# Raw-weight differences in a tile of their own from group 0 on, two eviction adds a group by DMA, two differences moved behind a sum

## The chip, the cores and the metric

One core of a Trainium2 chip. Its engines run side by side, each through its own list of instructions in order: TensorE (PE; its weight loads are shown as PEld), VectorE (DVE), ScalarE (ACT), GpSimd (POOL) and SyncE (SP). SP, ACT and POOL also issue DMAs. The metric is the device time of one execution in microseconds (us), here the median of several runs of the same kernel.

## What is computed

Attention with a window and a few global tokens, followed by a mixture of eight experts whose routing weights P are balanced by eight rounds of row and column normalisation:

```python
h = np.maximum(x @ w1[e], 0.0)     # x: 4352 x 512, w1[e]: 512 x 1024
ye = h @ w2[e]                     # w2[e]: 1024 x 512
out += P[:, e:e + 1] * ye          # over the eight experts
```

There are B = 8 batches with 544 rows each, so 4352 tokens reach the experts. The output is fp32, 4352 x 512. Products are made in fp16 with fp32 sums.

## The kernel before, in words

The first part, up to about 390 us, is the attention, the routing and, in the gaps, the first layer (x @ w1, ReLU) of experts 0 to 3, whose results are kept in DRAM as `hd`. The change does not touch it.

The second part is a loop over `units` (m, e): token groups m = 0 to 8 (eight of 512 tokens, one of 256), and in each group the experts in the order 4, 0, 5, 1, 6, 2, 7, 3. Units at even places are experts 4 to 7, whose first layer is still to do; at odd places stand experts 0 to 3, whose h is loaded from `hd` and scaled by P. Work goes in pairs: the even unit's turn runs its own second layer and, in between, the first layer of the even unit after it.

The second layer of a unit is seven products of half-size matrices in place of eight (`product(i, q)`, q = 1 to 7). `sums` makes what they need beside h itself on VectorE: part 0 and 1 are sums of quarters of h (tile s), part 2 is two differences written into h in place; products 6 and 7 read those differences, products 3 and 4 do not. Products 1 to 5 are summed over all experts of the group in fixed PSUM banks; products 6 and 7 of an even unit and of the odd unit after it share a rotating bank, which is then added into the group's output tile `o` by `add` (one quarter of `o` each). `add` is called at odd units for q = 6 and 7, and for all q when the group closes. The first expert pair sets its quarter of `o` with a scaling on ScalarE (L950), later ones add on VectorE (L952). `store` sends `o` out by POOL's queue.

The first layer comes in two forms. The plain one is `l1` (L819 to L827): weights `w1s`, 1 MB, in one of the two buffers of `wpool` with the tag w1e. The fast one (`Fast`, from group 2 on, experts 5, 6 and 7) also uses seven products in place of eight, in two halves p = 0 and 1; its weights `w1q` hold four raw blocks and three differences or sums of them, which are made once, written to DRAM (`w1c`), and loaded from there by every later group. `Fast.s1` and `Fast.s2` have one VectorE sum each, from PSUM to PSUM (L868, L875); `sums_x` makes differences of the scaled x.

Where the seven blocks of `w1c` are made is what the change is about. Before: for experts 6 and 7 a raw half is loaded by SP into a w1e buffer as an extra entry of the load sequence `wseq`, ahead of the w1s of units 10, 12, 14 and 16; `prep_w1` (four VectorE instructions) follows in the even units of group 1, and POOL writes the tile to `w1c`. For expert 5 the raw halves are loaded by POOL's queue into a tile of its own (`wq`, one buffer) at units 8 and 11 and are prepared in units 9 and 13. `load_w1` issues the next entry of `wseq` as soon as the entry two places before it is marked as used.

The scheduling of instructions is by hand: on each engine they stand in the order in which the loop records them. POOL has little else to do in this part: it issues the loads of the second-layer weights `w2c` for experts 2, 7 and 3 near 394 us, the loads and writes around `wq`, and the stores of `o`. SP issues, in each even unit, the loads of P rows (`pb`), of x (`xg`, once a group), of `h`, and of first-layer weights.

Of the kernel before, what the change touches and what calls it, by code (L numbers as in the profile page):

```python
# [9 lines left out]
FP16 = mybir.dt.float16  # L10
FP32 = mybir.dt.float32
AF = mybir.ActivationFunctionType
ALU = mybir.AluOpType
# [10 lines left out]
def kernel(  # L24
# [13 lines left out]
    nc = tc.nc  # L38

    B, H, Sl, Dh = q_l.shape  # L40
    Sg = q_g.shape[2]
    D, E = moe_w_gate.shape
    F = moe_w1.shape[2]
    P = 128
# [28 lines left out]
    WX = {5: 2, 6: 2, 7: 2}  # L73
# [18 lines left out]
    with tc.tile_pool(name="att_c", bufs=1) as att_c, \  # L92
# [161 lines left out]
        for so in range(NJ):  # L254
            for c0, n in ((W, P), (W + Sl, W // NJ)):
                nc.vector.tensor_copy(out=zsel[:, so, c0 : c0 + NJ * n].rearrange("p (x s) -> p x s", s=NJ)[:, :, so],
                                      in_=identity[:, 0:n])
# [330 lines left out]
        for s in range(HP, NU + 1):  # L588
            slot = s
            b, hp = divmod(s, HP)  # L590
# [101 lines left out]
    def tt(out, in0, in1, op):  # L692
        nc.vector.tensor_tensor(out=out, in0=in0, in1=in1, op=op)  # L693
# [14 lines left out]
    def fast(i):  # L708
        return i < NUN and units[i][0] < B and units[i][0] >= WX.get(units[i][1], B)

    wseq = [(i, p) for i in range(0, NUN, 2) for p in ((0, 1) if fast(i) else (None,))]
    for j, (e, p) in enumerate((e, p) for e in WX if e != 5 for p in range(2)):
        wseq.insert(next(k for k, w in enumerate(wseq) if w[0] == E + (2, 4, 6, 8)[j]), (e, "raw", p))
    raw = {}
    wnext = 0

    def load_w1(used):
        nonlocal wnext
        while wnext < len(wseq) and (wnext < 2 or wseq[wnext - 2] in used):
            i, *p = wseq[wnext]  # L720
            if p[0] is None:
                w = w1s[i] = wpool.tile([P, DP, F], FP16, tag="w1e", name="w1s")
                nc.sync.dma_start(out=w, in_=w1d[units[i][1] - NL])
            else:
                w = wpool.tile([P, 7, 2, 256], FP16, tag="w1e", name="w1q")
                if p[0] == "raw":
                    load_raw(i, p[1], w, nc.sync)
                    raw[wseq[wnext]] = w
                else:
                    nc.sync.dma_start(out=w, in_=w1c[units[i][1]][p[0]])  # L730
                    w1s[(i, p[0])] = w
            wnext += 1
            if wnext < 2:
                return

    def load_raw(e, p, w, eng):
        for o, r, k in ((0, 0, 0), (1, 0, 1), (3, 1, 0), (2, 1, 1)):
            f0 = 512 * r + 256 * p
            eng.dma_start(out=w[:, o], in_=w1d[e - NL][:, 2 * k : 2 * k + 2, f0 : f0 + 256])

    def prep_w1(ks=()):
        for k in ks or list(raw):
            w = raw.pop(k)
            for o, a, b, op in ((5, 0, 3, ALU.subtract), (3, 3, 2, ALU.add), (4, 3, 0, ALU.subtract),
                                (6, 1, 4, ALU.subtract)):
                tt(w[:, o], w[:, a], w[:, b], op)
            nc.gpsimd.dma_start(out=w1c[k[0]][k[2]], in_=w)
            used.add(k)

    def load_pb(*us):  # L750
        us = [i for i in us if i < NUN]
# [189 lines left out]
    def add(i, q, pm):  # L941
        m, e = units[i]
        nt = groups[m][1] // P // 2
        if m not in os_:
            os_[m] = ypool.tile([P, NJ, D], FP32, tag="y", name="o")
        for j, (r, d, sg) in enumerate(QUARTER[q]):
            o = os_[m][:, nt * r : nt * (r + 1), HD * d : HD * (d + 1)]
            p = pm[:, 0 : HD * nt].rearrange("p (t d) -> p t d", d=HD)
            if (q >= 6 and e == ORDER[1]) or (q in (3, 4) and j == 0):
                nc.scalar.mul(o, p, 1.0 / float(E))  # L950
            else:
                nc.vector.scalar_tensor_tensor(out=o, in0=p, scalar=sg / float(E), in1=o, op0=ALU.mult, op1=ALU.add)  # L952
# [130 lines left out]
    for i, (m, e) in enumerate(units):  # L1083
        if i == 2 * E - 2:
            wqx.close()
            fsp = ctx.enter_context(tc.tile_pool(name="fsp", bufs=1, reuse_waits="tile"))
        if i in (E, E + 3):
            k = (5, "own", int(i > E))
            own = wqp.tile([P, 7, 2, 256], FP16, tag="wq", name="wq")
            load_raw(k[0], k[2], own, nc.gpsimd)  # L1090
        if i == NUN - 1:
            last_pair(i)
        elif i % 2 == 0:
            alloc_h(i + 2)
            load_pbs(i)
            if (i + 4) % E == 0:
                load_x((i + 4) // E)
            load_h(i + 3)
            load_w1(used)
            if fast(i):  # L1100
                sums(i, 2, 4)
            if fast(i + 2):
                f = Fast(i + 2, 0)
                if fast(i):
                    product(i, 3)
                    f.s0()
                    product(i, 4)
                    f.s1()
                    sums_x(i + 2, (4,))
                    product(i, 5)  # L1110
                    product(i, 2)
                    f.s2()
                    sums(i + 1, part=(1,))
                    sums(i + 1, part=(0, 2))
                else:
                    f.s0()
                    product(i, 3)
                    f.s1()
                    scale_h(i + 1, HF, HF + 2)
                    for q in (4, 5, 2):  # L1120
                        product(i, q)
                    f.s2()
                    scale_h(i + 1, HF + 2, FT)
                    sums(i + 1)
                used.add((i + 2, 0))
                if fast(i):
                    scale_x(i + 4, 0, 2)
                else:
                    scale_x(i + 4)
                    scale_h(i + 3, 0, HF)  # L1130
                product(i, 1)
                f.s3()
                nrot = 0
                product(i, 6)
                product(i, 7)
                continue
            if i + 2 < NUN:
                sums(i + 1)
            else:
                n = groups[m][1]  # L1140
                h = hs[i + 1]
                s = ss[i + 1] = xsp.tile([P, HF, n], FP16, tag="xs", name="sl")
                tt(s, h[:, 0:HF, 0:n], h[:, HF:FT, 0:n], ALU.add)
            if m > 0:
                prep_w1()
            scale_x(i + 4)
            if m == 0:
                for e in {2: (2,), 4: (7,), 6: (3,)}.get(i, ()):
                    prep_w2c(e)
            sums_x(i + 4)  # L1150
            scale_h(i + 3, 0, HF if fast(i + 4) else FT)
            for fm in range(3):
                l1(i + 2, fm, ps_rot, rot())
            for q, fm in ((3, 3), (4, 4), (5, 5), (2, 6), (1, 7), (6, None), (7, None)):
                product(i, q)
                if fm is not None:
                    l1(i + 2, fm, ps_rot, rot())
                if closes(i):
                    add(i, q, fixed[q])
            used.add((i + 2, None))  # L1160
        else:
            if i >= E * B - 1:
                load_h(i + 4)
            load_w1(used)
            load_pbs(i)
            if fast(i + 1):
                f = Fast(i + 1, 1)
                late = fast(i - 1)
                if not late:
                    product(i, 3)  # L1170
                for q in (6, 7):
                    product(i, q)
                    add(i, q, fixed[q])
                if late:
                    scale_x(i + 3, 2, 4)
                    scale_h(i + 2, 0, HF)
                if late:
                    product(i, 3)
                f.s0()
                product(i, 4)  # L1180
                f.s1()
                sums_x(i + 3, (5,))
                product(i, 5)
                product(i, 2)
                sums(i + 1, 0, 2, part=(0, 1))
                f.s2()
                sums(i + 1, 0, 2, part=(2,))
                scale_h(i + 2, HF, FT)
                sums_x(i + 3, (7, 6))
                product(i, 1)  # L1190
                f.s3()
                used.add((i + 1, 1))
                nrot = 0
                continue
            if m > 0:
                sums(i + 1)
            if i in (E + 1, E + 5):
                raw[k] = own
                prep_w1((k,))
            for q in (6, 7, 3, 4, 5, 2, 1):  # L1200
                product(i, q)
                if q >= 6 or closes(i):
                    add(i, q, fixed[q])
                if q == 7 and m == 0:
                    sums(i + 1)
            if closes(i):
                store(m)
# [31 lines left out]
```

## Time and profile before

| | us |
|---|---|
| runs, median of 3 | 1034.1 (1033.37 to 1034.63) |
| profiled execution, device time | 1033.45 |
| its span in the profile | 1031.3 |
| PE busy | 1004.4 |
| DVE busy | 896.5 |
| ACT busy | 521.6 |
| POOL busy | 146.3 |

The granted TensorE clock is 0.998 of full speed over the span. From 400 to 1000 us the engines' busy times in stretches of 50 us are 49.0 to 50.0 for PE, 41.6 to 49.2 for DVE and 12.5 to 18.9 for ACT. Rows of the order of time give a start, the time covered, engine, line, operation, what is written and read, shape and count; in brackets stands the idle time of the engine before it and what ended it. A matmul's end is modelled in the profile, so consecutive matmuls overlap in it; distances between starts show the pace.

### The profile page before, as it was taken

How to read it: one execution, taken by the hardware profiler on the slowest of the kernel's cores; microseconds unless marked ns; L12 is line 12 of the kernel's file. 1: busy time of each engine (PE TensorE's matmuls, PEld its weight loads, DVE VectorE, ACT ScalarE, POOL GpSimd, SP SyncE). 2: the span in 40 equal slices, each digit the busy share in tenths (PEclk: the TensorE clock that was granted, in tenths of full speed). 3: DMA queues.
4: the chain of work that ended last, by engine and by line, in shares of the span. 5: the costliest groups of instructions: out<-in, count | busy, mean ns of one | idle time of the engine just before them, and what ended most of it. 6: DMA issues, size and time to landing. Idle time of an engine off the chain costs nothing.

```text
span 1031.3 us, 23197 instructions
## 1 busy us (share of the span) xinstructions
PE 1004.4 (97%) x9286; PEld 739.9 (72%) x9286; DVE 896.5 (87%) x1752; ACT 521.6 (51%) x1316; POOL 146.3 (14%) x237
## 2 busy tenths in 40 slices
PE   7899999999999999999999999999999999999998
PEld 4555555555555466777678878878878878888887
DVE  8688877877875768989889999999999999999996
ACT  7767888888886674322223334334333333433331
POOL 7442332423403002001100000000000000000000
PEclk9999999999999999999999999999999999999999
DMA  9897699989946989837866556555655645645650
GB/s 269 192 221 215 125 272 217 200 247 214 207 163 171 283 292 294 235 103 248 305 252 234 190 176 229 194 180 190 205 184 188 218 175 201 212 172 184 210 196 25
DMA packets 103499, 213.72 MB, mean 207 GB/s; under 512 B 34192, under 2 KB 68448, under 8 KB 92896
## 3 DMA queue, kind: packets, MB, share of 16 engines
q1 hardware_dynamic: 56928, 167.47, 47.5%
q0 software_dynamic: 43856, 35.14, 18.9%
q10 hardware_dynamic: 2608, 9.64, 2.4%
q8 instruction: 72, 1.18, 0.4%
q14 instruction: 35, 0.29, 0.1%
HBM read 174.41 MB, written 59.12 MB: 226 GB/s over the span
## 4 chain that ended last, share of the span: by engine, by line
PE 79%; DVE 9%; ACT 6%; issue 3%; DMA 2%; POOL 0%; SPq 0%; ACTq 0%; DVEq 0%; POOLq 0%
PE m L936 25%; PE ph L468 18%; PE pf L843 10%; PE pm L936 10%; PE ph L825 9%; ACT Pu L311 2%; DVE Pu L348 2%; DVE h L693 1%; PE pt L275 1%; ACT qbd L285 1%; DVE s L693 1%; DVE o L952 1%; PE ptw L359 1%; PE po L380 1%; ACT hT L471 1%
## 5 line engine op out<-in xcount | busy, mean ns | idle before, releaser
L468 PE MATMUL ph<-xT,w1e 128*128 128x512 f16 (+1 forms) x1152 | 259.8, 367 | 2.6 <-ACT hT L471 1.3
L936 PEld LDWEIGHTS <-h 128*128 128x128 f16 x2160 | 210.0, 98 | 35.7 <-DVE h L693 2.2
L936 PE MATMUL m<-w2c,s 128*128 128x256 f16 x1620 | 199.9, 273 | 0.0
L936 PEld LDWEIGHTS <-s 128*128 128x128 f16 x1620 | 158.2, 98 | 27.0
L468 PEld LDWEIGHTS <-w1e 128*128 128x128 f16 x1152 | 105.1, 98 | 97.9 <-issue 8.8
L827 ACT ACTIVATE h<-ph 128x512 f16<-128x512 f32 (+1 forms) x144 | 78.9, 550 | 152.3 <-PE ph L825 144.6
L693 DVE TENSOR_TENSOR h<-h,pb 128x2048 f16<-128x2048 f16 (+2 forms) x66 | 155.1, 2349 | 0.8 <-DMA h<-hd 0.8
L850 ACT ACTIVATE h<-pf 128x512 f16<-128x512 f32 x144 | 82.7, 596 | 123.2 <-PE pf L843 111.2
L693 DVE TENSOR_TENSOR s<-h 128x1024 f16<-128x1024 f16 (+2 forms) x178 | 127.7, 759 | 16.4 <-ACT h L827 8.6
L936 PE MATMUL m<-w2c,h 128*128 128x256 f16 x1080 | 138.2, 273 | 0.0
L825 PE MATMUL ph<-xs,w1s 128*128 128x512 f16 (+1 forms) x576 | 127.3, 355 | 1.5 <-DMA w1s<-w1d 1.5
L936 PE MATMUL pm<-w2c,h 128*128 128x256 f16 x1080 | 124.8, 273 | 0.5
L471 ACT ACTIVATE hT<-ph 128x512 f16<-128x512 f32 (+1 forms) x188 | 102.0, 558 | 38.2 <-PE ph L468 35.2
L843 PEld LDWEIGHTS <-w1q 128*128 128x128 f16 x1008 | 98.5, 98 | 11.9
L311 ACT ACTIVATE Pu<-ms,mx 128x160 f16<-128x160 f32 x224 | 93.3, 424 | 3.8 <-DVE mx L308 3.1
L473 DVE TENSOR_SCALAR hT<-ph 128x512 f16<-128x512 f32 x100 | 67.7, 687 | 28.1 <-PE ph L468 28.0
L693 DVE TENSOR_TENSOR h<-h 128x1024 f16<-128x1024 f16 (+1 forms) x178 | 91.7, 557 | 0.4
L693 DVE TENSOR_TENSOR xs<-xg,pb 128x1024 f16<-128x1024 f16 (+2 forms) x48 | 79.8, 1663 | 7.5 <-DMA pb<-pd 7.5
L825 PEld LDWEIGHTS <-w1s 128*128 128x128 f16 x576 | 56.2, 98 | 39.6 <-DMA w1s<-w1d 2.0
L955 POOL DMA_DIRECT2D out_dram<-o x8 | 6.1, 757 | 530.1 <-DVE o L952 530.1
L843 PE MATMUL pf<-xs,w1q 128*128 128x256 f16 x576 | 80.5, 272 | 0.0
L308 DVE CUSTOM_DVE_ANT_0 ms<-sc,mask 128x160 f32<-128x160 f32 x224 | 59.2, 318 | 9.6 <-PE sc L303 9.5
(168 smaller groups left out, 1248.2 us busy)
## 6 DMA issues: line engine op xcount, KB each, us to landing
h<-hd SPq DMA_DIRECT2D x32, 1024.0 KB
w1q<-w1c SPq DMA_DIRECT2D x36, 896.0 KB
hd<-hT SPq DMA_DIRECT2D x26, 1024.0 KB
w1s<-w1d SPq DMA_DIRECT2D x18, 1024.0 KB
pb<-pd SPq DMA_DIRECT2D x64, 256.0 KB
w2c<-in_moe_w_dram POOLq DMA_DIRECT2D x16, 512.0 KB, 22.2
out_dram<-o POOLq DMA_DIRECT2D x8, 1024.0 KB, 4.6
f<-in_q_l_dram SPq DMA_DIRECT2D x15, 512.0 KB
```

Source lines behind the costliest of these rows:

```text
L308: nc.vector.tensor_tensor_reduce(out=ms[:, ii, :], in0=sc[:, SW * ii : SW * (ii + 1)], in1=mask[:, mi, :], scale=-scale, scalar=BIG, op0=A ...
L311: nc.scalar.activation(out=d["Pu"][:, i, :], in_=ms[:, ii, :], func=AF.Exp, scale=-1.0, bias=d["mx"][:, i : i + 1], accum_out=d["sm"][:, i ...
L348: nc.vector.tensor_tensor(out=d["Pu"][:, i0:i1, 0:KW], in0=d["Pu"][:, i0:i1, 0:KW], in1=d["rs"][:, i0:i1].unsqueeze(2).to_broadcast([P, i1 ...
L468: nc.tensor.matmul(ph[:, 0:n], wts[e][:, dk, P * fm : P * (fm + 1)], xT[m][:, dk, :], start=(dk == 0), stop=(dk == DP - 1))
L471: nc.scalar.activation(out=hT[:, fm, 0:n], in_=ph[:, 0:n], func=AF.Relu)
L473: nc.vector.tensor_scalar(out=hT[:, fm, 0:n], in0=ph[:, 0:n], scalar1=0.0, scalar2=None, op0=ALU.max)
L693: nc.vector.tensor_tensor(out=out, in0=in0, in1=in1, op=op)
L825: nc.tensor.matmul(ph[:, 0:n], w1s[i][:, dk, P * fm : P * (fm + 1)], xss[i][:, dk, 0:n], start=(dk == 0), stop=(dk == DP - 1))
L827: nc.scalar.activation(out=hs[i][:, fm, 0:n], in_=ph[:, 0:n], func=AF.Relu)
L843: nc.tensor.matmul(bank[:, 256 * c : 256 * (c + 1)], self.w[:, self.sta[q], k, P * c : P * (c + 1)], self.mov[q][:, k], start=(first and c ...
L850: nc.scalar.activation(out=self.h[:, k : k + 2, 256 * c : 256 * (c + 1)], in_=bank.rearrange("p (k t) -> p k t", k=2), func=AF.Relu)
L936: nc.tensor.matmul(pm[:, HD * t : HD * (t + 1)], lhs[0][:, k, lhs[1] + P * t : lhs[1] + P * (t + 1)], w[:, k, q - 1, :], start=(k == 0 and ...
```

## The change

Three things change in the second part.

First, the raw halves of experts 5, 6 and 7 are all loaded by POOL's queue into the one tile `wq`, at units 0, 4, 6, 8, 10 and 12 (`RAW`), and are prepared at units 3, 5, 7, 9, 11 and 13, in the odd unit ahead of its products. The entries of `wseq` for raw halves, and the calls of `prep_w1` in even units, are gone. Three of the six preparations now lie in group 0.

Second, in groups 2 to 7 `add` for q = 6 and the experts at places 3 to 5 of the order is a scaling on ScalarE into a buffer `a` (one buffer, 128 x 2 x 256 fp32) and a DMA of POOL's queue that adds `a` into `o`. The places 3 to 5 are experts 1, 6 and 2; expert 6 stands at an even place, so there are two such DMAs a group.

Third, where a fast unit is followed by a fast pair, part 2 of `sums(i, 2, 4)`, two differences of h, stands behind `sums_x(i + 2, (4,))` instead of ahead of product 3. Nothing is changed in which products TensorE makes or in their order.

```diff
-    for j, (e, p) in enumerate((e, p) for e in WX if e != 5 for p in range(2)):
-        wseq.insert(next(k for k, w in enumerate(wseq) if w[0] == E + (2, 4, 6, 8)[j]), (e, "raw", p))
+    RAW = {0: (5, 0, 3), 4: (5, 1, 5), 6: (6, 0, 7), 8: (6, 1, 9), 10: (7, 0, 11), 12: (7, 1, 13)}
...
-                if p[0] == "raw":
-                    load_raw(i, p[1], w, nc.sync)
-                    raw[wseq[wnext]] = w
-                else:
-                    nc.sync.dma_start(out=w, in_=w1c[units[i][1]][p[0]])
-                    w1s[(i, p[0])] = w
+                nc.sync.dma_start(out=w, in_=w1c[units[i][1]][p[0]])
+                w1s[(i, p[0])] = w
...
-    def prep_w1(ks=()):
-        for k in ks or list(raw):
-            w = raw.pop(k)
-            for o, a, b, op in ((5, 0, 3, ALU.subtract), (3, 3, 2, ALU.add), (4, 3, 0, ALU.subtract),
-                                (6, 1, 4, ALU.subtract)):
-                tt(w[:, o], w[:, a], w[:, b], op)
-            nc.gpsimd.dma_start(out=w1c[k[0]][k[2]], in_=w)
-            used.add(k)
+    def prep_w1(i):
+        for e, p, u in RAW.values():
+            if u == i:
+                w = raw.pop((e, p))
+                for o, a, b, op in ((5, 0, 3, ALU.subtract), (3, 3, 2, ALU.add), (4, 3, 0, ALU.subtract),
+                                    (6, 1, 4, ALU.subtract)):
+                    tt(w[:, o], w[:, a], w[:, b], op)
+                nc.gpsimd.dma_start(out=w1c[e][p], in_=w)
...
-            if (q >= 6 and e == ORDER[1]) or (q in (3, 4) and j == 0):
+            if q == 6 and e in ORDER[3:6] and 2 <= m < B:
+                a = acp.tile([P, 2, HD], FP32, tag="a", name="a")
+                nc.scalar.mul(a, p, sg / float(E))
+                nc.gpsimd.dma_start(out=o, in_=a, accum_op=ALU.add)
+            elif (q >= 6 and e == ORDER[1]) or (q in (3, 4) and j == 0):
...
-        if i in (E, E + 3):
-            k = (5, "own", int(i > E))
-            own = wqp.tile([P, 7, 2, 256], FP16, tag="wq", name="wq")
-            load_raw(k[0], k[2], own, nc.gpsimd)
+            acp = ctx.enter_context(tc.tile_pool(name="acp", bufs=1, reuse_waits="tile"))
+        if i in RAW:
+            e1, p1, _ = RAW[i]
+            raw[(e1, p1)] = wqp.tile([P, 7, 2, 256], FP16, tag="wq", name="wq")
+            load_raw(e1, p1, raw[(e1, p1)], nc.gpsimd)
...
             if fast(i):
-                sums(i, 2, 4)
+                sums(i, 2, 4, part=(0, 1))
+                if not fast(i + 2):
+                    sums(i, 2, 4, part=(2,))
             if fast(i + 2):
...
                     f.s1()
                     sums_x(i + 2, (4,))
+                    sums(i, 2, 4, part=(2,))
                     product(i, 5)
...
-            if m > 0:
-                prep_w1()
+            prep_w1(i)
             scale_x(i + 4)
...
-            if i in (E + 1, E + 5):
-                raw[k] = own
-                prep_w1((k,))
+            prep_w1(i)
             for q in (6, 7, 3, 4, 5, 2, 1):
```

## The prediction

> **What bounds the kernel now.** I read the page's totals first, then busy time by stretch, then TensorE's order of time. From the page:
>
> ```profile
> span 1031.3 us, 23197 instructions
> PE 1004.4 (97%) x9286; PEld 739.9 (72%) x9286; DVE 896.5 (87%) x1752; ACT 521.6 (51%) x1316; POOL 146.3 (14%) x237
> ```
>
> VectorE at 87% could pass for a second bound, so I cut two neighbouring groups of 512 tokens out of the late part. Columns: busy us and count of PE, PEld, DVE, ACT, POOL, then clock, DMA share, GB/s.
>
> ```profile
> 546.00:620.48 74.48, 74.39 (x650) 63.13 (x649) 71.57 (x98) 27.39 (x48) 0.76 (x1) 1.00 0.57 195
> 620.48:694.96 74.48, 74.40 (x650) 63.12 (x649) 71.69 (x98) 27.40 (x48) 0.77 (x1) 1.00 0.58 196
> ```
>
> Both last 74.48 us, and PE lacks 0.09 us in each. VectorE lacks 2.8 to 2.9 us, yet it delays PE by next to nothing. So taking work from VectorE is worth only what PE loses by waiting, and the matmuls stay the same, in number and order. The whole question is how much PE waits after 365 us, and what new wait appears. I read each loss from start to start: a row's last start is its end less 0.27 us, the next is due 0.109 us later (24 matmuls in 2.78 us: 2.51 / 23).
>
> The large losses are the first matmuls of layer 1 in group 1 (PE, order of time):
>
> ```profile
> 485.74 2.46 PE L936 MATMUL m<-w2c,s 128*128 128x256 f16 x21
> 489.20 1.47 PE L825 MATMUL ph<-xs,w1s 128*128 128x512 f16 x6 [1.00 <-DMA w1s<-w1d]
> ...
> 505.72 2.78 PE L936 MATMUL m<-w2c,s 128*128 128x256 f16 x24
> 508.97 0.82 PE L825 MATMUL ph<-xs,w1s 128*128 128x512 f16 x3 [0.47 <-DMA w1s<-w1d]
> ```
>
> Due at 488.04 and begun at 489.20: 1.16 us. Due at 508.34 and begun at 508.97: 0.63 us. Together 1.8 us, both ended by the landing of w1s.
>
> The small ones come back in each of the six groups 2 to 7:
>
> ```profile
> 556.75 0.71 PE L936 MATMUL m<-w2c,h 128*128 128x256 f16 x5
> 557.54 0.72 PE L936 MATMUL pm<-w2c,h 128*128 128x256 f16 x5
> ...
> 586.81 0.60 PE L843 MATMUL pf<-xs,w1q 128*128 128x256 f16 x4
> 587.28 0.60 PE L843 MATMUL pf<-t,w1q 128*128 128x256 f16 x4
> 587.72 1.91 PE L936 MATMUL m<-w2c,s 128*128 128x256 f16 x16
> 589.50 0.70 PE L843 MATMUL pf<-xs,w1q 128*128 128x256 f16 x5
> ```
>
> 0.24, 0.03 and 0.03 us: 0.3 a group.
>
> **Part 1: raw weights leave SP's queue and PE's weight buffers.** Before, a raw half of w1 takes one of the two buffers that w1s uses. SP's DMA issues:
>
> ```profile
> 461.23 0.32 SPq L723 DMA_DIRECT2D w1s<-w1d  x1
> ...
> 484.23 0.33 SPq L723 DMA_DIRECT2D w1s<-w1d  x1
> ```
>
> The issue at 484.23 is for the matmuls due at 488.04. After, nothing raw stands between, so each w1s takes the buffer that comes free one unit pair earlier: this load goes out at 461.2, 27 us ahead. The longest such transfer in the chain of waits took 7.33 us:
>
> ```profile
> 501.60 7.33 DMA w1s<-w1d
> ```
>
> Both waits go: -1.8 us. SP also loses sixteen issues of raw loads, which only helps the loads behind them. What hides the w1s load is its lead of 27 us; without it the 1.8 us would stay.
>
> **Part 2: three of the six blocks of differences move into group 0.** A block is four VectorE instructions on one tile. Each of units 3, 5 and 7 gets a block ahead of its two additions from PSUM. VectorE there, with the idle time before an instruction in brackets, then the block (the row of w1q), and PE's first matmul into the bank that the closing additions free:
>
> ```profile
> 421.17 4.42 DVE L693 TENSOR_TENSOR h<-h,pb 128x4096 f16<-128x4096 f16 x1
> 425.67 0.69 DVE L952 SCALAR_TENSOR_TENSOR o<-pm,o 128x512 f32<-128x512 f32 x1
> 426.53 0.69 DVE L952 SCALAR_TENSOR_TENSOR o<-pm,o 128x512 f32<-128x512 f32 x1 [0.17 <-PE pm L936]
> 430.83 1.23 DVE L693 TENSOR_TENSOR s<-h 128x2048 f16<-128x2048 f16 x1 [0.67 <-PE m L936]
> 444.73 0.69 DVE L952 SCALAR_TENSOR_TENSOR o<-pm,o 128x512 f32<-128x512 f32 x1 [1.31 <-PE pm L936]
> 445.60 0.69 DVE L952 SCALAR_TENSOR_TENSOR o<-pm,o 128x512 f32<-128x512 f32 x1 [0.18 <-PE pm L936]
> 449.96 1.83 DVE L693 TENSOR_TENSOR s<-h 128x2048 f16<-128x2048 f16 x2 [0.74 <-PE m L936]
> 463.86 0.69 DVE L952 SCALAR_TENSOR_TENSOR o<-pm,o 128x512 f32<-128x512 f32 x1 [1.31 <-PE pm L936]
> 464.73 0.69 DVE L952 SCALAR_TENSOR_TENSOR o<-pm,o 128x512 f32<-128x512 f32 x1 [0.18 <-PE pm L936]
> 468.28 3.87 DVE L952 SCALAR_TENSOR_TENSOR o<-m,o 128x512 f32<-128x512 f32 x6
> ...
> 476.20 1.80 DVE L693 TENSOR_TENSOR w1q<-w1q 128x512 f16<-128x512 f16 x4
> ...
> 471.49 1.04 PE L936 MATMUL m<-w2c,h 128*128 128x256 f16 x8
> ```
>
> The gaps: 0.08 + 0.17 + 0.67 + 1.31 + 0.18 + 0.74 + 1.31 + 0.18 = 4.64 us. Without a gap an instruction starts 0.08 us before the last one ends (588.08 + 0.76 against a successor at 588.75, in part 3's rows), so eight filled gaps hold 5.3 us. Three blocks cost 3 x 1.72 = 5.2. If the weights are there, VectorE reaches the additions at 468.28 as before (0.1 us early). The first of these ends at 468.97, and PE needs its bank at 471.49: the cover is 2.5 us. Nearer in time, unit 3's two additions end 1.7 us later, at 428.1 and 428.9; PE needs their banks for the second and third product of layer 1 after unit 3's last matmul (430.81, the wait that ends at 430.83), each some 0.9 us long (six matmuls in 1.47 us above, four a product), so from 431.7 on.
>
> But the first block adds a wait, and VectorE stands in order behind it: the additions, s and h for the next units, xs. The raw half is loaded by POOL right behind six loads of w2c in the same queue. The view of w2c's loads, the stretch after their last landing, the view of the line that loads raw weights, and the row of DMA issues that writes a finished block out (KB, us to landing):
>
> ```profile
> L689 POOL DMA_DIRECT2D w2c<-in_moe_w_dram x6: 747/775/797, 394.4 to 398.1; - x6
> DMA to landing us min/median/max: 10.9/21.0/26.9
> ...
> 424.50:434.00 9.50, 9.50 (x78) 7.37 (x77) 8.58 (x12) 1.77 (x3) 0.00 (x0) 1.00 0.83 318
> ...
> L739 POOL DMA_DIRECT2D wq<-w1d x8: 702/721/732, 474.4 to 498.6; - x8
> DMA to landing us min/median/max: 2.7/4.4/6.6
> ...
> w1c<-wq POOLq DMA_DIRECT2D x2, 896.0 KB, 7.0
> ```
>
> The last w2c lands at 398.1 + 26.9 = 425.0. Call T the time at which the last of the four raw loads lands. VectorE is ready at 425.5, and the block's second instruction, 0.46 us on, needs that load. So VectorE loses T - 426.0, is 0.1 us less late at the closing additions, and PE loses T - 428.6 where that is positive. Bounds for T: 425.0 (they land with the last w2c) and 434, when SP's loads of this stretch, which hold the DMA engines at 0.83, are through. By the nearest row such loads take 2.7 to 6.6 us, median 4.4. I take 4.0, since they are queued already: T = 429.0, a loss of 0.4 us; the ends are 0 and 5.4. Unit 3's additions, 3.0 us later still, then end by 431.1 and 431.9, wanted from 431.7 and 432.6: in time. Units 5 and 7 have no such wait: POOL writes the block out and loads the next half in 7.0 + 6.6 us at most, and 19 us lie between blocks. In group 1 VectorE has three blocks fewer, 5.2 us, and makes up what is left.
>
> **Part 3: a third party for two additions a group.** For experts 1 and 2 of groups 2 to 7, 12 times in all (the third name in that slice, expert 6, stands at an even place, which never adds), ScalarE scales PSUM into a buffer and POOL adds it by DMA. VectorE loses 0.6 us each, ScalarE gains about the same:
>
> ```profile
> 576.60 1.28 DVE L952 SCALAR_TENSOR_TENSOR o<-pm,o 128x512 f32<-128x512 f32 x2
> 588.08 0.76 DVE L693 TENSOR_TENSOR h<-h 128x512 f16<-128x512 f16 x2
> 588.75 0.69 DVE L868 TENSOR_TENSOR pf<-pf,c 128x512 f32<-128x512 f32 x1
> 618.26 1.29 DVE L952 SCALAR_TENSOR_TENSOR o<-pm,o 128x512 f32<-128x512 f32 x2
> ...
> 578.32 0.57 ACT L859 COPY pf<-pf 128x512 f32<-128x512 f32 x1 [4.25 <-PE pf L843]
> ```
>
> ScalarE idles 4.25 us before its next copy, which covers it. The accumulating DMA isn't in the trace; the raw and w2c rows bound it by 2.7 and 26.9 us. I take 4.4, because POOL's queue is empty there and DMA share is 0.57. The same quarter is next added by VectorE at 618.26, 41 us after the first of two. Only near 26.9 would the single buffer hold ScalarE back for some 8 us at the second expert. VectorE runs about 0.25 us earlier (the second addition still waits for its matmul), enough for the 0.03 at 587.28.
>
> **Part 4: two differences behind a sum.** The pair at 588.08 (0.67 us) goes behind the sum at 588.75 and the t after it. PE waits for that sum at 589.50, so that 0.03 goes too; the differences feed only products 6 and 7, later, and the work behind them on VectorE starts no later. The 0.24 at 557.54 stays: its work starts from PE's own result. Parts 3 and 4: 6 x 0.06 = -0.4 us.
>
> **Sum.** -1.8 - 0.4 + 0.4 = -1.8 us. The profiled run is 1033.45 us, its span and 2.15 around it; that gives 1031.65. The median of the runs is 0.65 above it, so the forecast is 1034.1 - 1.8 = **1032.3 us**.
>
> **Rivals.** *The first half lands in time* (T up to 428.6): no loss, 1034.1 - 2.2 = 1031.9. For it: the least landing of the row, 2.7 us; against it: SP's loads at 0.83 share. *Halved rate*: the four loads alternate with SP's, take twice the least of the row, 5.4 us; T = 430.4, loss 1.8, 1033.7. The Trainium skill, "DMA: Bandwidth & Descriptors", section "Queues, rings and completion order", says each DMA engine takes turns packet by packet among its queues; by that rule T depends on packet sizes, and no quoted row shows the turns. *Slower*: the loads come after SP's transfers, T = 434, at VectorE's first block in unit 3; loss 5.4, 1037.3. It decides from T = 432.9 on (428.6 + 2.2 + 2.1). For it: POOL's w2c loads took up to 26.9 us in such a crowd; against it: w2c did progress while SP's loads ran. *POOL's issues hold VectorE up*: 0.76 us twice a group eats what VectorE saves; parts 3 and 4 give nothing, 1032.7. Against it: the block at 476.20 ran while POOL issued raw loads (from 474.4 on, 0.72 each) and took 1.80 us, 0.45 an instruction. The Trainium skill, "SBUF — State Buffer", section "SBUF: two separate sides", states such an exclusive lock; that row does not show it.
>
> **Numbers.** Chances: forecast 0.45, in time 0.25, halved 0.12, slower 0.10, POOL 0.05, others 0.03. About 0.2% (2.1 us) is what a measurement of this kernel tells from no change: faster means under 1032.0, slower over 1036.2. The forecast falls under 1032.0 three times in ten, "in time" two in three: faster 0.33; slower 0.13; within 0.54. The range runs from 1031.9 less the 0.7 by which single runs lie off their median, to the loss of 3.0 us that the longest landing of the row would bring (T = 425.0 + 6.6): 1031.2 to 1034.9.
>
> **What would show it.** Right: no wait of PE for w1s, blocks of 1.8 us in units 3, 5 and 7, the first begun only near 428, PE held under 1 us near 471, ScalarE's 12 scalings inside its idle time, late groups of 74.4 us. Wrong: the first block ending after 434, PE waiting for VectorE's closing additions by several us, late groups longer than 74.5, or w1s waits still there.

## The result, and the profile after

| | before | changed |
|---|---|---|
| median of 17 runs each, us | 1033.8 (1032.8 to 1035.12) | 1031.68 (1030.66 to 1033.76) |
| ratio to before, 95% interval | | 0.9981 [0.9974, 0.9988] |
| profiled execution, us | 1033.45 | 1031.69 |

0.9981 of 1033.8 us is a gain of 2.0 us. The interval, 1.2 to 2.7 us, lies wholly on the side of faster, and it holds the 0.2% (2.1 us) from which the prediction counts a kernel as faster: which side of that line the change lies on is not decided by these runs. The page of the changed kernel, totals:

```profile
PE 1004.5 (98%) x9286; PEld 741.1 (72%) x9286; DVE 891.1 (87%) x1740; ACT 528.7 (51%) x1328; POOL 172.2 (17%) x265
```

PE has the same 9286 matmuls and the same busy time. The twelve additions have left VectorE (1752 to 1740 instructions; its busy time falls by 5.4 us) and come back as 7.1 us of ScalarE and, as DMA issues, on POOL, which with the 16 raw loads taken over from SP has 25.9 us more.

The opening of the program, which the change does not touch, does not always last equally long, so spans are poor for a difference of 2 us. I compare the second part alone, from PE's first row of the experts' first layer to its last row of the program. PE's order of time, before and then changed:

```profile
385.46 5.77 PE L825 MATMUL ph<-xs,w1s 128*128 128x512 f16 x26
...
1026.40 0.60 PE L969 MATMUL pm<-w2c,sl 128*128 128x256 f16 x4
```

```profile
386.63 4.70 PE L820 MATMUL ph<-xs,w1s 128*128 128x512 f16 x21
...
1025.34 0.60 PE L968 MATMUL pm<-w2c,sl 128*128 128x256 f16 x4
```

From start to start 640.94 us before and 638.71 after: 2.23 us less. The opening of this execution took 1.17 us more; times of the changed trace are 1.17 later than those of before for the same work.

Where the two waits for w1s were, PE now has (changed kernel, order of time):

```profile
486.59 2.78 PE L931 MATMUL m<-w2c,s 128*128 128x256 f16 x24
489.21 2.11 PE L820 MATMUL ph<-xs,w1s 128*128 128x512 f16 x9
...
505.72 2.78 PE L931 MATMUL m<-w2c,s 128*128 128x256 f16 x24
508.34 2.75 PE L820 MATMUL ph<-xs,w1s 128*128 128x512 f16 x12
```

Due at 486.59 + 2.78 - 0.27 + 0.11 = 489.21, and begun at 489.21; the second likewise, 508.34. SP's issue of the w1s for the first of them, at 484.23 before, stands here:

```profile
462.41 0.32 SPq L722 DMA_DIRECT2D w1s<-w1d  x1
```

The six late groups, PE again:

```profile
555.78 1.04 PE L931 MATMUL m<-w2c,h 128*128 128x256 f16 x8
556.90 1.92 PE L931 MATMUL pm<-w2c,h 128*128 128x256 f16 x16
...
586.16 0.60 PE L838 MATMUL pf<-xs,w1q 128*128 128x256 f16 x4
586.60 0.60 PE L838 MATMUL pf<-t,w1q 128*128 128x256 f16 x4
587.04 1.91 PE L931 MATMUL m<-w2c,s 128*128 128x256 f16 x16
588.78 1.04 PE L838 MATMUL pf<-xs,w1q 128*128 128x256 f16 x8
...
631.31 1.92 PE L931 MATMUL pm<-w2c,h 128*128 128x256 f16 x16
```

The matmuls from 586.16 on follow each other without a gap (586.60 is 0.44, four matmuls, after 586.16; 588.78 is 1.74, sixteen, after 587.04): both losses of 0.03 are gone. At 556.90 the row is still 0.24 late (555.78 + 1.04 - 0.27 + 0.11 = 556.66). One group, 556.90 to 631.31, now takes 74.41 us in place of 74.48.

The first block of differences, VectorE in the changed kernel; then the lines on the raw loads and on w2c's loads (least, median and longest time to landing):

```profile
422.35 4.42 DVE L693 TENSOR_TENSOR h<-h,pb 128x4096 f16<-128x4096 f16 x1
427.70 1.82 DVE L693 TENSOR_TENSOR wq<-wq 128x512 f16<-128x512 f16 x4 [0.93 <-DMA wq<-w1d]
...
446.06 1.79 DVE L693 TENSOR_TENSOR wq<-wq 128x512 f16<-128x512 f16 x4
...
464.40 1.80 DVE L693 TENSOR_TENSOR wq<-wq 128x512 f16<-128x512 f16 x4
...
470.25 5.07 DVE L951 SCALAR_TENSOR_TENSOR o<-m,o 128x512 f32<-128x512 f32 x8
```

```profile
L689 POOL DMA_DIRECT2D w2c<-in_moe_w_dram x6: 747/766/785, 395.6 to 399.3; - x6
...
DMA to landing us min/median/max: 10.3/21.1/27.1
```

The block waits 0.93 us for the raw weights. The last w2c landed at 399.3 + 27.1 = 426.4; the block ran through in 1.82 us, as long as the blocks without a wait, so the last raw load was there when the second instruction came, 0.44 us after 427.70, at most 1.8 us behind the last w2c. The view of these four loads agrees: issued from 400.0 to 409.4, they took 26.8 to 18.7 us to landing, which puts the first at 426.8 and the last at 428.1. The closing additions start at 470.25, and the first ends near 470.9. PE's row that needs its bank:

```profile
472.67 1.04 PE L931 MATMUL m<-w2c,h 128*128 128x256 f16 x8
```

Nothing of the wait reaches PE.

### The profile page after: what moved, and what is told of

It is laid out like the page before. It is cut to its first block, busy times and chain, and to the rows that moved or that the text cites. A ratio compares the mean times of both kernels' runs of the same rounds, so it can differ in the third digit from the quotient of the medians.

```text
span 1029.9 us, 23231 instructions
## 1 busy us (share of the span) xinstructions
PE 1004.5 (98%) x9286; PEld 741.1 (72%) x9286; DVE 891.1 (87%) x1740; ACT 528.7 (51%) x1328; POOL 172.2 (17%) x265
## 4 chain that ended last, share of the span: by engine, by line
PE 83%; DVE 8%; ACT 6%; issue 2%; DMA 1%; SPq 0%; POOL 0%; ACTq 0%; DVEq 0%
PE m L931 27%; PE ph L468 18%; PE ph L820 11%; PE pm L931 10%; PE pf L838 10%; ACT Pu L311 2%; DVE Pu L348 2%; DVE h L693 1%; ACT qbd L285 1%; PE ptw L359 1%; PE pt L275 1%; DVE s L693 1%; PE po L380 1%; ACT hT L471 1%; DMA vraw<-in_v_l_dram 1%
## 5 line engine op out<-in xcount | busy, mean ns | idle before, releaser
L838 PE MATMUL pf<-t,w1q 128*128 128x256 f16 x432 | 64.8, 273 | 0.0
```

The lines of the kernel that those rows point to most:

```text
L838: nc.tensor.matmul(bank[:, 256 * c : 256 * (c + 1)], self.w[:, self.sta[q], k, P * c : P * (c + 1)], self.mov[q][:, k], start=(first and c ...
```

## Experiments

The table has one line for each kernel run. "Second part" is the distance between the same two rows as above, in the profiled execution; "against before" is that less 640.94.

| kernel | time, us | ratio to before | second part, us | against before |
|---|---|---|---|---|
| changed | 1031.68 | 0.9981 [0.9974, 0.9988] | 638.71 | -2.23 |
| e1, first change only | 1032.16 | 0.9982 [0.9973, 0.9991] | 639.14 | -1.80 |
| e2, second and third only | 1033.0 | 0.9991 [0.9982, 1.0] | 639.72 | -1.22 |
| e3, second only | 1032.72 (one) | | 640.56 | -0.38 |
| e4, third only | 1033.12 (one) | | 640.08 | -0.86 |
| e5, first block in unit 1 | 1045.8 (one) | | 652.84 | +11.90 |
| e6, q = 7 additions left out | 1031.79 | 0.9978 [0.9969, 0.9987] | 638.72 | -2.22 |
| e7, scaling split elsewhere | 1030.69 | 0.9972 [0.9963, 0.9982] | 637.16 | -3.78 |
| e8, first raw half earlier | 1031.62 (one) | | 638.71 | -2.23 |
| e9, first raw half later | 1033.31 (one) | | 641.55 | +0.61 |
| e10, changed again | 1032.47 | 0.9985 [0.9972, 0.9998] | 638.69 | -2.25 |
| e11, e7 again | 1029.82 | 0.9961 [0.9948, 0.9974] | 637.16 | -3.78 |

Beside e1, e2, e6 and e7 before took 1033.96 (32 runs), beside e3, e4, e5 and e8 1034.51 (one), beside e9 1033.84 (one), beside e10 and e11 1034.05 (14 runs).

**e1: the first change alone.** The changed kernel without the ScalarE and DMA branch and with `sums` in its old place:

```diff
-            if q == 6 and e in ORDER[3:6] and 2 <= m < B:
-                a = acp.tile([P, 2, HD], FP32, tag="a", name="a")
-                nc.scalar.mul(a, p, sg / float(E))
-                nc.gpsimd.dma_start(out=o, in_=a, accum_op=ALU.add)
-            elif (q >= 6 and e == ORDER[1]) or (q in (3, 4) and j == 0):
+            if (q >= 6 and e == ORDER[1]) or (q in (3, 4) and j == 0):
...
-            acp = ctx.enter_context(tc.tile_pool(name="acp", bufs=1, reuse_waits="tile"))
...
-                sums(i, 2, 4, part=(0, 1))
-                if not fast(i + 2):
-                    sums(i, 2, 4, part=(2,))
+                sums(i, 2, 4)
...
-                    sums(i, 2, 4, part=(2,))
```

> The raw-weight change alone. Theory (TensorE bounds the kernel, and the gain is its two waits for w1s in group 1): 1.8 us under the kernel before, ratio 0.9983; no wait of PE for w1s, the losses of 0.03 us twice a group stay, late groups of 74.48 us. Rival (VectorE's saved additions bring the gain): ratio 1.000.

Measured: 0.9982, and a second part 1.80 us shorter, which is the 1.16 + 0.63 of the two waits for w1s, with nothing taken off. In its late groups the small losses are still there (PE, order of time of e1, the one ahead of t's product):

```profile
586.20 0.60 PE L838 MATMUL pf<-xs,w1q 128*128 128x256 f16 x4
586.67 0.60 PE L838 MATMUL pf<-t,w1q 128*128 128x256 f16 x4
```

586.67 comes 0.47 after 586.20, not 0.44. So the first change removes the two large waits and only those, and the 0.43 between e1 and the changed kernel belongs to the other two.

**e2, e3, e4: the other two changes, together and singly.** The kernel before with (e2) both, (e3) the first edit below, (e4) the second:

```diff
-            if (q >= 6 and e == ORDER[1]) or (q in (3, 4) and j == 0):
+            if q == 6 and e in ORDER[3:6] and 2 <= m < B:
+                a = acp.tile([P, 2, HD], FP32, tag="a", name="a")
+                nc.scalar.mul(a, p, sg / float(E))
+                nc.gpsimd.dma_start(out=o, in_=a, accum_op=ALU.add)
+            elif (q >= 6 and e == ORDER[1]) or (q in (3, 4) and j == 0):
...
+            acp = ctx.enter_context(tc.tile_pool(name="acp", bufs=1, reuse_waits="tile"))
```

```diff
-                sums(i, 2, 4)
+                sums(i, 2, 4, part=(0, 1))
+                if not fast(i + 2):
+                    sums(i, 2, 4, part=(2,))
...
                     sums_x(i + 2, (4,))
+                    sums(i, 2, 4, part=(2,))
                     product(i, 5)
```

> The two additions a group by DMA and the moved differences, without the raw-weight change. Theory: 0.4 us under the kernel before, ratio 0.9996, late groups of 74.42 us, both waits for w1s still there (1.2 and 0.6 us). Rival (VectorE bounds the late groups): 12 x 0.68 = 8 us faster, ratio 0.992.

> Only the two additions a group by DMA. Theory: PE no longer loses 0.03 us ahead of the products of t (587.28 before), and still loses 0.03 us ahead of the product behind the sum (589.50 before), or less, since VectorE is some 0.25 us earlier. Rival (POOL's issues hold VectorE up as long as it saves): both losses stay.

> Only the two differences behind the sum. Theory: the loss of 0.03 us behind the sum goes, that ahead of the products of t stays.

Measured, e2 first: 0.9991, an interval that reaches 1.0; the runs alone do not tell 0.4 us from nothing. The traces do, after a correction: the second wait for w1s was not there in the profiled executions of e2 and e4, although both load their raw weights as before does, and it was there in that of e3. What PE waited for, e3 and then e4 (us, times, longest):

```profile
PE ph L825 <- DMA w1s<-w1d: 1.4, 2, 1.0
```

```profile
PE ph L825 <- DMA w1s<-w1d: 1.0, 1, 1.0
```

e3 with both waits is 0.38 us shorter than before: its second change is worth the 12 x 0.03 on which the prediction counted for both. PE in e3:

```profile
586.92 0.60 PE L843 MATMUL pf<-xs,w1q 128*128 128x256 f16 x4
587.35 0.60 PE L843 MATMUL pf<-t,w1q 128*128 128x256 f16 x4
587.79 1.91 PE L936 MATMUL m<-w2c,s 128*128 128x256 f16 x16
589.54 1.04 PE L843 MATMUL pf<-xs,w1q 128*128 128x256 f16 x8
```

There 587.35 and 589.54 are in pace (0.43 and 1.75 after the starts before them). In e4 the first of these losses stays and the second is gone:

```profile
586.77 0.60 PE L843 MATMUL pf<-xs,w1q 128*128 128x256 f16 x4
587.24 0.60 PE L843 MATMUL pf<-t,w1q 128*128 128x256 f16 x4
587.67 1.91 PE L936 MATMUL m<-w2c,s 128*128 128x256 f16 x16
589.42 1.04 PE L843 MATMUL pf<-xs,w1q 128*128 128x256 f16 x8
```

587.24 is 0.47 after 586.77; 589.42 is 1.75 after 587.67. So the moved differences buy the loss behind the sum, and the additions that left VectorE buy both. Of e4's 0.86 us, 0.63 is the wait that did not happen in that execution, which leaves 0.23. Of e2's 1.22, 0.63 is that wait too, and another 0.22 is its first wait, of 0.78 us in place of 1.00, which leaves 0.37. That is no more than e3 has with the second change alone: the two overlap, and with the second in place the third adds next to nothing.

**e6: more relief for VectorE.** The changed kernel without the q = 7 additions of experts 1 and 2 in groups 2 to 7, twelve VectorE instructions less:

```diff
-            else:
+            elif not (q == 7 and e in ORDER[3:6] and 2 <= m < B):
```

> The changed kernel, with the q = 7 additions of experts 1 and 2 in groups 2 to 7 left out altogether: VectorE has 12 instructions of 0.68 us less again, and the output lacks those products. Theory: nothing, 0.998 of the kernel before as the changed kernel, late groups of 74.41 us. Rival (VectorE's load sets the pace): 8 us faster than the changed kernel, ratio 0.990.

Measured: a second part of 638.72 us, as in the changed kernel. A late group, changed and then e6 (columns as in the prediction):

```profile
546.00:620.40 74.40, 74.32 (x651) 63.16 (x649) 70.76 (x96) 28.49 (x50) 3.22 (x3) 1.00 0.60 202
```

```profile
546.00:620.40 74.40, 74.32 (x650) 63.16 (x648) 69.47 (x93) 28.47 (x51) 3.22 (x3) 1.00 0.60 202
```

VectorE has 1.3 us less to do in the group, and PE's busy time in it is the same to 0.01 us. So VectorE's load as such bounds nothing here; what counted in e3 was that VectorE came earlier to the work for which PE waits.

**e8, e9: how late the first raw half may land.** e8 loads it ahead of the last six loads of w2c, e9 lets SP load it in unit 3:

```diff
+    raw[(5, 0)] = wqp.tile([P, 7, 2, 256], FP16, tag="wq", name="wq")
+    load_raw(5, 0, raw[(5, 0)], nc.gpsimd)
...
-            raw[(e1, p1)] = wqp.tile([P, 7, 2, 256], FP16, tag="wq", name="wq")
-            load_raw(e1, p1, raw[(e1, p1)], nc.gpsimd)
+            if i:
+                raw[(e1, p1)] = wqp.tile([P, 7, 2, 256], FP16, tag="wq", name="wq")
+                load_raw(e1, p1, raw[(e1, p1)], nc.gpsimd)
```

```diff
-    RAW = {0: (5, 0, 3), 4: (5, 1, 5), 6: (6, 0, 7), 8: (6, 1, 9), 10: (7, 0, 11), 12: (7, 1, 13)}
+    RAW = {3: (5, 0, 3), 4: (5, 1, 5), 6: (6, 0, 7), 8: (6, 1, 9), 10: (7, 0, 11), 12: (7, 1, 13)}
...
-        if i in RAW:
+        if i in RAW and i != 3:
...
+            if i == 3:
+                raw[(5, 0)] = wqp.tile([P, 7, 2, 256], FP16, tag="wq", name="wq")
+                load_raw(5, 0, raw[(5, 0)], nc.sync)
```

> The changed kernel with the first raw half loaded ahead of the last six w2c loads in POOL's queue. Theory: it lands near 405, VectorE's wait of 0.9 us ahead of the first block goes, PE's losses after 365 us stay at 2.3 us as in the changed kernel, so no change of time. Rival (the first block's wait still costs something): PE's losses fall.

> The changed kernel with the first raw half loaded by SP's queue in unit 3, behind the load of w1s and the P rows, and its block in the same unit. Call R the end of the scaling of h ahead of the block, T the landing of its last load. Theory (by the prediction's step: PE loses T - R - 3.0, since VectorE's gaps in group 0 hold three blocks and the closing additions have 2.5 us of cover): T - R of 3 to 6 us, and PE loses 0 to 3 us near 471, ahead of the first matmul of its first fixed bank in group 1, to within 0.5 us of that rule; w1s is still in time. Rival (a wait in unit 3 costs PE at once, through the rotating banks): PE loses about T - R less 1 us near 432.

Measured in e8, VectorE:

```profile
426.61 1.80 DVE L693 TENSOR_TENSOR wq<-wq 128x512 f16<-128x512 f16 x4
```

No wait is left, and the second part has the 638.71 us of the changed kernel: its 0.93 us of waiting cost nothing. In e9 the block waits longer, VectorE and then PE:

```profile
430.78 1.80 DVE L693 TENSOR_TENSOR wq<-wq 128x512 f16<-128x512 f16 x4 [5.47 <-DMA wq<-w1d]
```

```profile
433.24 1.89 PE L820 MATMUL ph<-xs,w1s 128*128 128x512 f16 x8 [1.86 <-DVE o L951]
...
474.05 1.03 PE L931 MATMUL m<-w2c,h 128*128 128x256 f16 x8 [0.66 <-DVE o L951]
```

VectorE waits 5.47 us and PE loses 2.84 against the changed kernel (from start to start 0.16 more than each bracket: 2.02 and 0.82). The prediction's rule (VectorE's loss less 2.6 us of slack) gives 5.47 - 2.6 = 2.9. The size is right, the place mostly not: PE waited 1.86 us at once, at 433.24, for unit 3's own additions and the rotating banks that they free, and only 0.66 at the closing additions.

**e5: a load that cannot be there.** The first block stands two units earlier:

```diff
-    RAW = {0: (5, 0, 3), 4: (5, 1, 5), 6: (6, 0, 7), 8: (6, 1, 9), 10: (7, 0, 11), 12: (7, 1, 13)}
+    RAW = {0: (5, 0, 1), 4: (5, 1, 5), 6: (6, 0, 7), 8: (6, 1, 9), 10: (7, 0, 11), 12: (7, 1, 13)}
```

> The changed kernel with the first block of differences in unit 1 in place of unit 3; its loads are issued as before. Theory (VectorE waits for the last raw load in order, and TensorE loses what exceeds VectorE's cover): the loads land near 428, VectorE waits for them from about 411 on, some 16 us, and PE loses 11 to 15 us in unit 2, where it waits for s; about 13 us over the changed kernel. Rival (the cover is large enough wherever the block stands, or loads come as they are asked for): within 2 us of the changed kernel.

Measured: a second part 14.13 us longer than the changed kernel's. VectorE, then PE, and a window of the same stretch (PE, PEld, DVE, ACT, POOL, clock, DMA share, GB/s):

```profile
427.46 1.80 DVE L693 TENSOR_TENSOR wq<-wq 128x512 f16<-128x512 f16 x4 [16.16 <-DMA wq<-w1d]
```

```profile
430.46 1.89 PE L931 MATMUL m<-w2c,s 128*128 128x256 f16 x8 [11.60 <-DVE s L693]
432.14 1.91 PE L820 MATMUL ph<-xs,w1s 128*128 128x512 f16 x4
433.84 1.75 PE L931 MATMUL m<-w2c,s 128*128 128x256 f16 x8
435.43 1.03 PE L820 MATMUL ph<-xs,w1s 128*128 128x512 f16 x4
```

```profile
430.00:434.00 4.00, 3.54 (x13) 1.94 (x14) 4.00 (x7) 0.00 (x0) 0.42 (x2) 0.50 0.56 229
```

VectorE waits 16.16 us for the raw weights. PE stands still for 11.60 us, and then runs at a granted clock of 0.50. The twenty matmuls from 430.46 to 435.43 take 4.97 us, where sixteen at 0.109 and four at 0.215 make 2.6: another 2.4 us. 11.6 + 2.4 is 14.0 of the 14.1. So there was cover even here, some 4.5 us between VectorE's wait and PE's, but all that exceeds it reaches PE at once, and a wait of this length costs PE more than itself.

**e7: the loss that stayed.** The 0.24 us at 556.90 stood in front of the product that reads the first difference of h, which VectorE makes behind a sum in PSUM (L870), a scaling of h and s. e7 takes one more slice of that scaling ahead of the sum, where VectorE is idle:

```diff
-                    scale_h(i + 1, HF, HF + 2)
+                    scale_h(i + 1, HF, HF + 3)
...
-                    scale_h(i + 1, HF + 2, FT)
+                    scale_h(i + 1, HF + 3, FT)
```

> The changed kernel, with three quarters in place of half of one scaling of h moved into VectorE's idle time of 1.23 us ahead of the sum in the first pair of a group. Theory (the 0.25 us that PE still loses there once a group is VectorE's work behind that sum): that wait goes, late groups of 74.17 us, 6 x 0.25 = 1.5 us under the changed kernel, about 0.9967 of the kernel before. Rival (the wait has another cause): 0.998 as the changed kernel, groups of 74.41 us.

VectorE in the changed kernel and in e7:

```profile
552.56 0.70 DVE L870 TENSOR_TENSOR pf<-pf,c 128x512 f32<-128x512 f32 x1 [1.23 <-PE pf L838]
553.16 1.22 DVE L693 TENSOR_TENSOR h<-h,pb 128x1024 f16<-128x1024 f16 x1
554.41 1.82 DVE L693 TENSOR_TENSOR s<-h 128x2048 f16<-128x2048 f16 x2
```

```profile
553.21 0.70 DVE L870 TENSOR_TENSOR pf<-pf,c 128x512 f32<-128x512 f32 x1 [0.70 <-PE pf L838]
553.81 0.68 DVE L693 TENSOR_TENSOR h<-h,pb 128x512 f16<-128x512 f16 x1
554.53 1.83 DVE L693 TENSOR_TENSOR s<-h 128x2048 f16<-128x2048 f16 x2
```

From the sum to s 1.85 us, then 1.32. PE in e7 goes from 556.43 to 557.30 without a gap (0.87 us for eight matmuls), and the second part is 1.55 us shorter than the changed kernel's: 6 x 0.25. The runs follow, 1030.69 against the changed kernel's 1031.68 in other runs. Both were then timed side by side, beside the same runs of before:

> The changed kernel as it is, on the same chip and beside the same runs of before as the next one. Theory (1.8 us of w1s waits and 0.4 us of small waits gone): a ratio of 0.9979 to 0.9981 to before, 1031.7 us. Rival (part of the first difference was the scatter of the opening 386 us): a ratio nearer to 0.9990.

> The split of the h scaling at HF + 3 in place of HF + 2, beside the changed kernel on the same chip. Theory (it takes 0.25 us of PE's wait out of each of six late groups): 1.0 to 1.5 us under the changed kernel, about 1030.5. Rival (the earlier difference between the two came from the opening of the runs): within 0.4 us of the changed kernel.

Measured: 1032.47 (11 runs) and 1029.82 (5 runs), ratios 0.9985 [0.9972, 0.9998] and 0.9961 [0.9948, 0.9974] to the same runs of before. In both pairs of profiles the second parts differ by 1.53 to 1.55 us, and the medians by 1.0 and 2.65; with openings that vary by up to 3 us between executions the size in the medians is loose, the direction is not. e10's ratio lies between its theory (0.9979 to 0.9981) and its rival (0.9990), and its interval holds both; its second part, 638.69 us, is that of the first profile. e7 is the fastest kernel here.

## Why the prediction came out as it did

The predicted 1032.3 us lay 0.6 over the measured 1031.68, inside its own range from 1031.2 to 1034.9. The median lies just under the 1032.0 from which the prediction speaks of faster, to which it gave 0.33, against 0.54 for a change too small to tell. By its steps:

- **What bounds the kernel: only PE's waits after 365 us.** Held: the second part went by the late starts of PE, one for one, in every kernel above (in e5 with the slow matmuls behind the wait), and e6 shows that relief for VectorE without such a wait is worth nothing.
- **Part 1, -1.8 us.** Right in cause and size: e1 alone gives -1.80, and w1s goes out 26.8 us ahead of its matmuls (462.41 to 489.21; predicted 27). That it comes to 0.01 us is in part luck. Of four profiled executions with the old loading, the first wait was 0.78 to 1.00 us long, and the second was there in two (before, e3) and not in the others (e2, e4); from a profile like those, the prediction would have counted 0.9 to 1.2 us. What decides on the second wait was not tried.
- **Part 2, +0.4 us.** This is the term that was mis-sized. The prediction took "T = 429.0, a loss of 0.4 us", four microseconds behind the last w2c. Measured: at most 1.8 behind, VectorE held for 0.93 us instead of 3.0, PE for nothing. The row that it took counts from the issue of a load; these four had spent that time behind w2c and came in within 1.3 us of each other (426.8 to 428.1). The rival "in time" is what happened, and the sum with it, -2.2, is the -2.23 of the trace. The rest of the reasoning on this part stands: the blocks of units 5 and 7 ran without a wait (rows at 446.06 and 464.40), and e9 bears out the price of a later landing. With a landing as late as in e9, though, the rotating banks of unit 3's additions are missed first. The prediction had the figures for this (an addition that ends at 428.1 without a wait and is wanted from 431.7 has 3.6 us of slack, so 1.9 of the 5.47 are lost there), but its rule named only the bank of the closing additions.
- **Parts 3 and 4, -0.4 us.** Right: -0.43 between e1 and the changed kernel. The share of part 4 is smaller than its place in the sum suggests, since e3 has both losses gone without it.
- **The 0.24 stays.** It did, in all six groups. Its work does start from PE's own result, as the prediction says, but e7 shows that 0.5 us of VectorE's scaling could go ahead of that result, and then it need not have stayed.
- **The accumulating DMA.** Taken at 4.4 us to landing; the view of its line in the changed kernel:

```profile
L947 POOL DMA_DIRECT2D o<-a x12: 1172/1185/1247, 576.3 to 966.7; - x12
...
DMA to landing us min/median/max: 3.9/4.0/5.2
```

4.0 us, and 5.2 at the longest, far from the 26.9 at which the one buffer would have held ScalarE.

- **The rival of POOL's issues.** Refuted by e3, where the additions by DMA alone took both small losses away. Each issue takes 1.19 us of POOL, longer than the 0.76 assumed, and still VectorE ran beside the one at 576.35 (1.25 us) at its usual pace:

```profile
574.82 1.22 DVE L693 TENSOR_TENSOR xs<-xg,pb 128x1024 f16<-128x1024 f16 x1
...
576.93 1.22 DVE L693 TENSOR_TENSOR xs<-xg,pb 128x1024 f16<-128x1024 f16 x1
```

The sum of the trace, 1033.8 - 2.2 = 1031.6, meets the measured median. Of the 0.6 by which the forecast missed, 0.4 is the term of part 2; before itself, with 17 runs, lies 0.3 under the median of three from which the forecast started.

## What to carry to other kernels

Where one engine is nearly always busy, list its late starts one by one and price a change only by those that it removes or makes; the busy share of another engine, even at 87%, says nothing by itself. A wait put into a second engine costs the first nothing up to the slack of what is queued behind it, and everything beyond (here 0.93, 5.47 and 16.16 us of VectorE's waiting cost PE 0, 2.8 and 14.1), so look for the first consumer of each instruction behind the wait, the nearest one in time too. And to measure 0.2%, compare the distance between two fixed instructions in the part that was changed: it repeated to 0.02 us here where PE waited for no landing (638.71, 638.69; 637.16 twice), while whole runs of one kernel spread over 3 us. Where PE does wait for a landing, as for w1s in the kernel before, one execution is not enough.

## What the runs showed of the hardware

In e5 PE stood still from 418.9 to 430.46. The mean granted clock was 0.65 from 418 to 430, 0.50 from 430 to 434 and 0.89 from 434 to 440; the trace has no values but 0.50 and 1.00 there, so it fell near 421.6, some 2.8 us after the last matmul, and came back near 435.3, 4.8 us after the first one behind the wait. Until then a matmul of 256 columns took about 0.21 us in place of 0.109. The Trainium skill, "TensorE: Matmul & The Clock Gate", section "Part 1: The HAM clock gate", says that the array falls to half rate once it has idled for a window of some 3.4 us and comes back after as long a busy stretch. The trace agrees on the half rate and roughly on the delays, 2.8 us on the way down and 4.8 us on the way up. In e5 this made a wait of 11.6 us dearer by 2.4; behind the wait of 1.86 us in e9 the granted clock was 1.00 (430 to 440).

The opening before PE's first row of the second part lasted 385.18 to 388.43 us in the profiled executions, 386.63 and 385.40 in two of the same kernel. What sets it was not tried.
